# Projecting Q and K of 14 tokens six steps ahead in a two-layer recurrent attention kernel

## The chip, the cores and the metric

The kernel runs on one core of one Trainium2 chip, in one launch. The metric is the device time of that core in microseconds. The kernel before took 1781.42 us (median of three runs, 1781.21 to 1782.36).

## The reference

Two kinds of layer are applied twice with the same weights: a segmented attention with a recurrent memory (A), then a gated MLP (B), each on a layer norm and with a residual. The data type is bfloat16, the sequence has 2048 tokens of width 512, there are 32 heads of width 128, a segment has 32 tokens and the memory 8.

```python
def _A_ref(x, mem0, Wq, Wk, Wv, Wo, seg_len):
    ...
    mask = (idx[:, None] < M) | (idx[:, None] >= idx[None, :])
    mem = mem0
    for s in range(n_seg):
        xs = x[:, s * seg_len:(s + 1) * seg_len, :].copy()
        h = jnp.concatenate([mem, xs], axis=1)
        q = jnp.einsum('btd,dhe->bhte', h, Wq)
        k = jnp.einsum('btd,dhe->bhte', h, Wk)
        v = jnp.einsum('btd,dhe->bhte', h, Wv)
        scores = jnp.einsum('bhqe,bhke->bhqk', q, k) * scale
        scores = jnp.where(mask[None, None], scores, -1000000000.0)
        p = _softmax(scores, axis=-1)
        o = jnp.einsum('bhqk,bhke->bhqe', p, v)
        o = jnp.einsum('bhte,hed->btd', o, Wo)
        mem = o[:, :M, :].copy()
        outs.append(o[:, M:, :])
    return jnp.concatenate(outs, axis=1)
def _B_ref(x, w_gate, w_up, w_down):
    ...
    h = _sigmoid(g) * u
    return jnp.einsum('bsf,fd->bsd', h, w_down)
x = A_x
x = x + _A_ref(_layernorm(x, axis=-1), A_mem0, A_Wq, A_Wk, A_Wv, A_Wo, A_seg_len)
x = x + _B_ref(_layernorm(x, axis=-1), B_w_gate, B_w_up, B_w_down)
x = x + _A_ref(_layernorm(x, axis=-1), A_mem0, A_Wq, A_Wk, A_Wv, A_Wo, A_seg_len)
x = x + _B_ref(_layernorm(x, axis=-1), B_w_gate, B_w_up, B_w_down)
```

The loop over the 64 segments is a chain: a segment can begin only when the memory of the one before it is there. The tokens of a segment do not depend on that chain in the first attention layer: there they are the normalised input.

## The kernel before

**Steps.** `trace` (L1152) runs 70 steps. Step t works on segment t of the first attention layer (layer 0) and on segment t-6 of the second (layer 1); the distance 6 is `LAG`. Steps 0 to 5 have layer 0 alone and 40 columns (8 memory, 32 tokens); steps 6 to 63 have both and 80 columns; steps 64 to 69 have layer 1 alone, 40 columns. The transposed activations of a step lie in one of 8 ring tiles `hT` (128 x 4 x 80): columns 0 to 31 are the tokens of layer 0, 32 to 39 its memory, 40 to 47 the memory of layer 1, 48 to 79 its tokens. In steps 0 to 5 the columns 40 to 79 hold zeros (L572).

**One step** (`emit_step`, L826). The 32 heads go in six groups, five of six heads and one of two. A group does its work in halves of three heads: Q and K by matmuls of the weights' 128x128 blocks with the columns of `hT` (L892: 3 heads x 2 x 4 = 24 matmuls a half, 256 a step, into one PSUM bank), a copy of the bank to a tile `qku` on ScalarE (L902, recorded at L1232), and the scores (L906). Then come mask, maximum, subtraction, exponential, sum, reciprocal and product on VectorE and ScalarE (L920 to L937), a transpose (L949), two copies to `ptsb` (L960, on either engine), the product with V (L975), a copy `otsb` on ScalarE (L983), and the output projection (L993, 128 matmuls a step). The first columns of its result are the memory of the next step; VectorE copies them to the next `hT` (L1006, L1011), and then the Q and K of the next step can begin. V of most tokens is projected ahead of time in passes of a whole 128-row tile (`v_pass`, L695, and `v_half`, L732), goes to DRAM (`scr`), and is loaded into `vsb` by SyncE's queue (L861). V of the memory and of the remaining tokens is projected in the step by "strips" of 32 columns (L817) and put into `vsb` by more transfers of that queue (L872).

**Work beside the chain.** After every fourth step the MLP of a block of 128 tokens is done (`ffn`, L1048): seven pairs of gate and up matmuls (L1095), each followed by a tanh on ScalarE into one of two tiles `th` (L1100) and a product on VectorE (L1102), and then the down projection (L1119). Its weights come from DRAM each time by GpSimd's queue (L1087, L1088, L1113). These tasks, the V passes and the layer norms (L651 to L664) are what TensorE has besides the chain.

**Start.** The weights and the first blocks of x are loaded by SyncE's queue (L591, L779, L794). Blocks 2 and 14 are normalised first (L1167), then 3, 4, 5, 7, then the memory's initial value is transposed (L637), then blocks 0 and 1 (`pre1`), then 8, 10, 11, 13. Meanwhile TensorE runs matmuls on a tile of zeros, `hot` (L1218)[...].

**Order.** Every task is added to a planner with the engines that may run it, a cost, and the keys it reads and writes. A string, `SEQUENCE`, gives every task a rank. `forward` (L272) then simulates the engines: each time an engine is free it takes the ready task of best rank for which its buffers are free. The program is emitted in the order of the planned starts, and the engines run it in that order. A copy with two possible engines goes to the one that is free first. `warm` (L415) adds the matmuls on zeros before tasks of TensorE for which the plan has a gap of over 250 ns. The string therefore sets the order of the whole program, not only of the part around a change.

Of the kernel before, what the change touches and what calls it, by code (L numbers as in the profile page):

```python
# [13 lines left out]
BF16 = mybir.dt.bfloat16  # L14
# [12 lines left out]
SCOL = 24  # L27
BLK = 4
# [430 lines left out]
class Kern:  # L459
# [366 lines left out]
    def emit_step(self, t):  # L826
# [13 lines left out]
        pl.rate = ncol / 2.4 / mm_ns(ncol)  # L840

        c0 = 0 if both else L * j0

        def mv(c):
            return hT[:, c, c0:c0 + ncol]

# [451 lines left out]
```

## Time and profile before

| | |
|---|---|
| median of three runs | 1781.42 us |
| span of the profiled execution, first to last instruction | 1781.3 us |
| TensorE matmul busy | 1754.0 us, 98% |
| TensorE weight load busy | 1517.1 us, 85% |
| VectorE busy | 1144.1 us, 64% |
| ScalarE busy | 1167.8 us, 66% |
| GpSimd busy | 573.8 us, 32% |
| granted TensorE clock | 1.000 |
| first Q and K matmul of step 0, 1, 6, 7, 8, 12 | 28.3, 85.5, 177.5, 204.3, 224.2, 327.6 us |
| Q and K matmuls (L892) | 14848 of 80 columns, 3072 of 40 |
| matmuls on zeros (L1218) | 109 |

The span covers all but 0.1 us of the median. Busy is the union of an engine's instruction times. Matmuls overlap in the pipeline, so the mean of about 200 ns of one matmul is its latency and not its cost; the cost of one in a row of many is the distance between starts, which is read from the chain of work by dividing the length of a piece by its count.

### The profile page before, as it was taken

The numbers are of one execution on the slowest core, as the hardware profiler recorded it, in microseconds if no ns is written. First come the engines' busy times: TensorE is split into PE (matmuls) and PEld (weight loads), VectorE is DVE, ScalarE is ACT, GpSimd is POOL, SyncE is SP. The second block draws the span as 40 slices with busy tenths as digits, with TensorE's granted clock in tenths as the row PEclk, the third lists the DMA queues.
The fourth block names the chain that finished last, engine by engine and source line by source line (L and its number), as shares of the span: only waits on it lengthen the run. The fifth ranks groups of instructions, "written<-read, shape, count | busy, mean of one in ns | idle before, by whom it ended". The sixth has DMA issues, their size and how long they took to land.

```text
span 1781.3 us, 91977 instructions
## 1 busy us (share of the span) xinstructions
PE 1754.0 (98%) x39873; PEld 1517.1 (85%) x40083; DVE 1144.1 (64%) x3931; ACT 1167.8 (66%) x2973; POOL 573.8 (32%) x828
## 2 busy tenths in 40 slices
PE   9999999999999999999999999999999999999998
PEld 4688888888888898989898898988888888989886
DVE  4376666776577666756666676657656665666675
ACT  6676666666666666666766666666666766667564
POOL 5314031513233242323324241333324232333332
PEclk9999999999999999999999999999999999999999
DMA  9825254635555464445546453555555454555543
GB/s 342 265 74 165 59 155 121 195 105 158 146 162 153 133 174 136 139 137 165 160 130 198 135 161 106 154 160 167 156 148 172 111 145 140 158 156 139 165 143 94
DMA packets 131943, 270.66 MB, mean 152 GB/s; under 512 B 30394, under 2 KB 65090, under 8 KB 131538
## 3 DMA queue, kind: packets, MB, share of 16 engines
q0 software_dynamic: 56240, 181.91, 34.7%
q1 hardware_dynamic: 75298, 82.86, 16.3%
q8 instruction: 314, 5.14, 1.3%
q14 instruction: 91, 0.75, 0.1%
HBM read 220.41 MB, written 25.69 MB: 138 GB/s over the span
## 4 chain that ended last, share of the span: by engine, by line
PE 91%; DVE 5%; ACT 2%; issue 1%; DMA 1%; SPq 1%; POOL 0%; ACTq 0%; DVEq 0%; POOLq 0%
PE bank L892 31%; PE bank L993 17%; PE bank L1095 11%; PE bank L695 8%; PE bank L817 7%; PE bank L975 4%; PE bank L906 4%; PE bank L1119 4%; PE bank L949 2%; DVE st L920 1%; PE bank L1218 1%; PE bank L664 1%; DVE small L925 1%; DVE small L932 1%; DVE st L927 1%
## 5 line engine op out<-in xcount | busy, mean ns | idle before, releaser
L892 PE MATMUL bank<-hT,wq_sb 128*128 128x80 bf16 (+1 forms) x8960 | 622.6, 198 | 1.3 <-issue 0.6
L892 PE MATMUL bank<-hT,wk_sb 128*128 128x80 bf16 (+1 forms) x8960 | 622.5, 198 | 0.6 <-issue 0.6
L1232 ACT CAST qku<-bank 128x480 bf16<-128x480 f32 (+3 forms) x770 | 388.3, 512 | 222.5 <-PE bank L892 142.0
L892 PEld LDWEIGHTS <-wq_sb 128*128 128x128 bf16 x8960 | 454.1, 99 | 35.0 <-issue 25.1
L892 PEld LDWEIGHTS <-wk_sb 128*128 128x128 bf16 x8960 | 450.8, 99 | 0.8 <-issue 0.7
L920 DVE TENSOR_TENSOR st<-bank,cst 40x240 f32<-40x240 f32 (+3 forms) x768 | 277.7, 367 | 200.9 <-PE bank L906 194.2
L993 PE MATMUL bank<-otsb,wo_sb 128*128 128x80 bf16 (+1 forms) x8960 | 362.8, 198 | 1.9 <-ACT otsb L1232 0.2
L993 PEld LDWEIGHTS <-wo_sb 128*128 128x128 bf16 x8960 | 336.7, 99 | 16.3 <-issue 1.9
L1087 POOL DMA_DIRECT2D wg<-in_B_w_gate_dram x217 | 164.0, 756 | 299.1 <-PE bank L1095 109.8
L1232 ACT CAST otsb<-bank 128x480 bf16<-128x480 f32 (+3 forms) x420 | 199.8, 482 | 59.6 <-PE bank L975 47.6
L1088 POOL DMA_DIRECT2D wu<-in_B_w_up_dram x217 | 163.9, 756 | 197.3 <-PE bank L1095 89.3
L1113 POOL DMA_DIRECT2D wd<-in_B_w_down_dram x217 | 153.8, 709 | 213.4 <-PE bank L906 74.5
L930 ACT ACTIVATE st<-st 80x240 f32<-80x240 f32 (+3 forms) x420 | 159.5, 381 | 39.9 <-DVE st L927 37.1
L654 POOL TENSOR_TENSOR small<-small,cst 128x1 f32<-128x1 f32 (+1 forms) x80 | 44.8, 562 | 413.7 <-DVE small L653 410.2
L1095 PE MATMUL bank<-xnT,wg 128*128 128x128 bf16 (+2 forms) x1784 | 172.0, 219 | 0.8
L1095 PE MATMUL bank<-xnT,wu 128*128 128x128 bf16 (+2 forms) x1784 | 171.2, 219 | 0.0
L906 PE MATMUL bank<-qku 128*128 128x80 bf16 (+1 forms) x2240 | 161.0, 198 | 1.5 <-ACT qku L1232 0.2
L932 DVE TENSOR_REDUCE small<-st 80x6 f32<-80x240 f32 (+3 forms) x420 | 150.6, 360 | 16.3 <-ACT st L930 14.0
L937 DVE TENSOR_TENSOR pb<-st,small 80x240 bf16<-80x240 f32 (+3 forms) x420 | 153.6, 368 | 4.2
L927 DVE TENSOR_TENSOR st<-st,small 80x240 f32<-80x240 f32 (+3 forms) x420 | 154.1, 368 | 3.1
L925 DVE TENSOR_REDUCE small<-st 80x6 f32<-80x240 f32 (+3 forms) x420 | 151.4, 362 | 4.6
L975 PE MATMUL bank<-ptsb,vsb 104*128 104x80 bf16 x2048 | 140.2, 199 | 3.0 <-DMA vsb<-sst 1.5
(102 smaller groups left out, 2345.2 us busy)
## 6 DMA issues: line engine op xcount, KB each, us to landing
wg<-in_B_w_gate_dram POOLq DMA_DIRECT2D x220, 256.0 KB, 4.3
wu<-in_B_w_up_dram POOLq DMA_DIRECT2D x220, 256.0 KB, 4.3
wd<-in_B_w_down_dram POOLq DMA_DIRECT2D x220, 256.0 KB, 4.3
vsb<-scr SPq DMA_DIRECT2D x460, 48.0 KB
vsb<-sst SPq DMA_DIRECT2D x464, 32.0 KB
scr<-vst SPq DMA_DIRECT2D x112, 96.0 KB
wv_sb<-in_A_Wv_dram SPq DMA_DIRECT2D x8, 512.0 KB
wo_sb<-in_A_Wo_dram SPq DMA_DIRECT2D x10, 384.0 KB
```

Of the source, the lines that this page charges most:

```text
L892: nc.tensor.matmul(o_ap, lhsT=W[:, c, h * P:(h + 1) * P], rhs=mv(c), start=(c == 0), stop=(c == DC - 1))
L906: nc.tensor.matmul(s_all(SB)[:, w0 + i, :], lhsT=fview(qku[:, i, 0, 0:1], [(1, P)]), rhs=qku[:, i, 1, 0:ncol], start=True, stop=True)
L920: pl.add("DVE", dve_ns(n, True), lambda gsz=gsz, hs=hs, st=st, SB=SB, pj_=pj_, npj_=npj_, mk=mk, idx=idx: nc.vector.tensor_tensor(out=st[p ...
L925: pl.add("DVE", dve_ns(n), lambda hs=hs, st=st, mx=mx: nc.vector.tensor_reduce(out=mx[pr, hs], in_=st[pr, hs], axis=AX.X, op=ALU.max), r=s ...
L927: pl.add("DVE", dve_ns(n), lambda gsz=gsz, hs=hs, st=st, mx=mx: nc.vector.tensor_tensor(out=st[pr, hs], in0=st[pr, hs], in1=mx[pr, hs].uns ...
L932: pl.add("DVE", dve_ns(n), lambda hs=hs, st=st, sm=sm: nc.vector.tensor_reduce(out=sm[pr, hs], in_=st[pr, hs], axis=AX.X, op=ALU.add), r=s ...
L975: nc.tensor.matmul(fview(OB[:, o:o + 1], [(ncol, 2), (1, L)]), lhsT=self.vsb[halves[u // 8]][0:64 + L, j, (u % 8) * P:(u % 8 + 1) * P], rh ...
L993: nc.tensor.matmul(WB[:, c * ncol:(c + 1) * ncol], lhsT=self.wo[:, h, c * P:(c + 1) * P], rhs=otsb[:, hl, 0:ncol], start=(h == 0 and c == ...
L1087: pl.add("POOL", 760, lambda wg=wg, fs=fs: nc.gpsimd.dma_start(out=wg[:], in_=self.wgv[:, :, fs]), r=[("wo", self.H - 1)], w=[gk] + bt, la ...
L1088: pl.add("POOL", 760, lambda wu=wu, fs=fs: nc.gpsimd.dma_start(out=wu[:], in_=self.wuv[:, :, fs]), r=[("wo", self.H - 1)], w=[uk] + bt, la ...
L1095: nc.tensor.matmul(gu[:, 2 * i + k, 0:n], lhsT=W[:, c, i * P:(i + 1) * P], rhs=xnT[:, c, rw], start=(c == 0), stop=(c == DC - 1))
L1232: nc.scalar.copy(out=dst, in_=src)
```

## The change

The columns 40 to 79 of `hT`, which steps 0 to 5 leave unused, get 14 tokens of the segment that is six steps away. `early_x` copies the first 14 normalised tokens of segment t+6 into columns 40 to 53 of step t's tile, for t = 0 to 5 (from block 1 for t = 0 and 1, from block 2 for t = 2 to 5). In steps 0 to 5 the Q and K matmuls take 54 columns. The first 40 go to `qku` as before. The other 14 columns of each head go to a tile `kx` (128 x 32 x 2 x 14), by one more copy per half group on ScalarE or VectorE, and from there to a DRAM tensor `xq`, in two transfers a step on SyncE's queue. In steps 6 to 11 the two parts are loaded back into the same tile `kx`; the matmuls take columns 14 to 79, 66 in place of 80; the copy of the bank fills columns 14 to 79 of `qku`, and one more copy per half group, from `kx`, fills columns 0 to 13. The second tile `th` of the MLP is gone; the one that is left is a pool of the planner. The string `SEQUENCE` is another one, so that all instructions stand in a new order. In the new order the initial memory is transposed first, and the blocks of x are loaded in another order. Counted over the program, TensorE has 1536 matmuls of 66 columns and 1536 of 54 where it had 1536 of 80 and 1536 of 40, and 85 matmuls on zeros for 109; ScalarE and VectorE have 66 copies into `kx` (59 and 7), 66 out of it (46 and 20), and 6 into `hT` (4 and 2) more; SyncE's queue has 24 transfers more; all else is the same in number.

```diff
+NE = 14
...
 SEQUENCE = r"""
...
+        self.kx = c.tile([P, H, 2, NE], BF16, name="kx")
+        self.xq = dr.tile([self.LAG * P, H * 2 * NE], BF16, name="xq")
         self.hff = [c.tile([P, FC, P], BF16, name=f"hff{i}") for i in range(1)]
-        self.th = [c.tile([P, 2, P], F32, name=f"th{i}") for i in range(2)]
+        self.th = [c.tile([P, 2, P], F32, name=f"th{i}") for i in range(1)]
...
+        self.thp = Pool(self.th)
...
+    def early_x(self, pst, B, b):
+        for i in range(BLK):
+            t = b * BLK + i - self.LAG
+            if 0 <= t < self.LAG:
+                dst = self.hT[t % self.R][:, :, L:L + NE]
+                self.pl.add(("ACT", "DVE"), copy_ns(4 * NE, True), lambda dst=dst, i=i: (dst, pst()[:, :, i * SEG:i * SEG + NE]),
+                            r=[B], w=[("hT", t % self.R, 1, q) for q in ("m", "x")])
...
+            if b == 2:
+                self.early_x(pst, B, b)
...
+        save, load = t < LAG, LAG <= t < 2 * LAG
+        q0, q1 = (0, L + NE) if save else (NE, ncol) if load else (c0, c0 + ncol)
+        nq = q1 - q0
+        parts, pos = ((0, self.H // 2 + 2), (self.H // 2 + 2, self.H)), 0
+        if load:
+            for lo, hi in parts:
+                w = NE * 2
+                pl.add("SP", 430, lambda lo=lo, hi=hi, w=w: nc.sync.dma_start(out=fview(self.kx[:, lo, 0, 0:1], [(1, (hi - lo) * w)]),
+                                                                             in_=self.xq[(t - LAG) * P:(t - LAG + 1) * P, lo * w:hi * w]),
+                       r=[("xq", t - LAG, lo)], w=[("kx", p) for p in range(lo, hi)], lat=3000.0, nb=P * (hi - lo) * w * 2)
+
         def mv(c):
-            return hT[:, c, c0:c0 + ncol]
+            return hT[:, c, q0:q1]
...
-                            o_ap = pq[:, (2 * i + qk_) * ncol:(2 * i + qk_ + 1) * ncol]
+                            o_ap = pq[:, (2 * i + qk_) * nq:(2 * i + qk_ + 1) * nq]
...
+                d0 = NE if load else 0
+                nw_ = ncol - d0
                 def qkcopy(nh=nh, pq=pq, qku=qku):
-                    return (fview(qku[:, 0, 0, 0:1], [(LW, 2 * nh), (1, ncol)]),
-                            pq[:, 0:2 * nh * ncol].rearrange("p (m b) -> p m b", b=ncol))
+                    return (fview(qku[:, 0, 0, d0:d0 + 1], [(LW, 2 * nh), (1, nw_)]),
+                            pq[:, 0:2 * nh * nq].rearrange("p (m b) -> p m b", b=nq)[:, :, 0:nw_])
...
+                if load:
+                    pl.add(("ACT", "DVE"), copy_ns(2 * nh * NE, True), lambda nh=nh, qku=qku, kxv=kxv: (fview(qku[:, 0, 0, 0:1], [(LW, 2 * nh), (1, NE)]), kxv()),
+                           r=kk, w=[(qku, "e")], use=[qku])
...
+                if save:
+                    pl.add(("ACT", "DVE"), copy_ns(2 * nh * NE), lambda nh=nh, pq=pq, kxv=kxv: (kxv(), pq[:, 0:2 * nh * nq].rearrange("p (m b) -> p m b", b=nq)[:, :, L:nq]),
+                           r=[pq], w=kk)
+                pos += nh
+                for lo, hi in parts:
+                    if save and pos == hi:
+                        w = NE * 2
+                        pl.add("SP", 430, lambda lo=lo, hi=hi, w=w: nc.sync.dma_start(out=self.xq[t * P:(t + 1) * P, lo * w:hi * w],
+                                                                                     in_=fview(self.kx[:, lo, 0, 0:1], [(1, (hi - lo) * w)])),
+                               r=[("kx", p) for p in range(lo, hi)], w=[("xq", t, lo)], lat=3000.0, nb=P * (hi - lo) * w * 2)
...
-            hi2 = self.nxt("th", 2)
-            th = self.th[hi2]
+            th = pl.buf(self.thp)
...
         p1 = self.pre1(1)
+        self.early_x(*p1, 1)
```

## The prediction, made before the changed kernel ran

> **What bounds the kernel now.** I read the page first, then the windows by step, then the chain of waits, and last the timeline where a step looked short of work.
>
> ```profile
> span 1781.3 us, 91977 instructions
> PE 1754.0 (98%) x39873; PEld 1517.1 (85%) x40083; DVE 1144.1 (64%) x3931; ACT 1167.8 (66%) x2973; POOL 573.8 (32%) x828
> PE 91%; DVE 5%; ACT 2%; issue 1%; DMA 1%; SPq 1%; POOL 0%; ACTq 0%; DVEq 0%; POOLq 0%
> ```
>
> TensorE is idle for 27.3 us in all, and 91% of the chain that ended last is its matmuls. So a matmul that becomes shorter is worth its whole saving wherever other TensorE work stands ready. Busy alone doesn't say what a matmul costs; the chain does, by length over count:
>
> ```profile
> 69.75 2.40 PE bank L892 x96
> ...
> 177.69 3.44 PE bank L892 x96
> 181.24 2.58 PE bank L892 x72
> ```
>
> 40 columns: 2.40/96 = 25.0 ns. 80 columns: 3.44/96 = 2.58/72 = 35.83 ns. And 128 columns, at 241 us:
>
> ```profile
> 244.39 0.90 PE bank L1095 x16
> ```
>
> 0.90/16 = 56 ns. Now the steps that the change touches: the start, steps 1 to 5, then 6, 7 and 8 (columns: stretch, its length, then busy us of PE, weight loads, DVE, ACT, POOL, then clock, DMA share, GB/s):
>
> ```profile
> 0.00:28.30 28.30, 27.07 (x146) 12.55 (x149) 11.52 (x44) 17.33 (x28) 16.29 (x46) 1.00 0.98 324
> ...
> 85.50:177.50 92.00, 89.38 (x2583) 75.62 (x2587) 62.38 (x221) 60.74 (x202) 25.52 (x36) 1.00 0.43 120
> 177.50:204.30 26.80, 26.54 (x556) 20.97 (x559) 14.64 (x52) 17.93 (x42) 0.00 (x0) 1.00 0.26 69
> 204.30:224.20 19.90, 18.93 (x479) 17.57 (x475) 12.80 (x48) 13.92 (x34) 0.00 (x0) 1.00 0.18 46
> 224.20:251.60 27.40, 27.22 (x624) 25.11 (x626) 18.70 (x65) 16.67 (x41) 11.89 (x17) 1.00 0.52 150
> ```
>
> Steps 6 and 8 last 27 us because V passes and the MLP fill them; step 7 lasts 19.9 us and is the only one with nothing to fill it (no L695, no L1095, 1.3 us of zeros). There VectorE is the bound: it starts at 208.27 and then works without a gap to 221.1.
>
> ```profile
> 208.27 0.84 DVE L920 TENSOR_TENSOR st<-bank,cst 80x240 f32<-80x240 f32 x2 [5.85 <-PE bank L906]
> ...
> 220.90 0.24 DVE L1226 TENSOR_SCALAR ptsb<-bank,small 104x80 bf16<-104x80 bf16 x1
> ```
>
> At the start TensorE multiplies zeros; the first normalised block is ready at 9.31 + 0.40 = 9.71 us, but its transposes come at 11.98, behind 43 of them:
>
> ```profile
> 1.00 11.14 PE L1218 MATMUL bank<-hot 128*128 128x512 bf16 x43 [1.00 <-DVE small L564]
> 11.98 0.39 PE L664 MATMUL bank<-cst,xn 128*128 128x128 bf16 x4
> ```
> ```profile
> 9.31 0.40 DVE L655 TENSOR_SCALAR xn<-xs,small 128x512 bf16<-128x512 bf16 x1
> ```
>
> **What the Trainium skill says.** (1) "TensorE: Matmul & The Clock Gate", section "Wait — 56ns, not 53.3ns?": back to back and warm, a matmul of N columns takes N/2.4 + 2.5 ns, never under about 25 ns. The trace agrees at 80 (35.83), 128 (56) and at the floor (25.0 for 40). (2) "ScalarE: Activation LUTs", section "What ACT_TABLE_LOAD costs": 186 ns + 0.833 ns an element with immediates, and back-to-back instructions overlap by 93 ns. The trace has the slope, (557-358)/240 = 0.83, and a little less fixed time. (3) "DMA: Bandwidth & Descriptors", section "Specifications": full rate wants pieces of 512 B or more. The new transfers have rows of 784 and 1008 B; no row of this trace tests that.
>
> **The change part by part.** The sum is made against the profiled span, 1781.3 us; 0.1 us lies around it to the median, 1781.42.
>
> *a. 66 columns for 80, steps 6 to 11.* 6 x 32 heads x 2 x 4 = 1536 matmuls. No 66 is in the trace. By (1) it is 30.0 ns; the slope between 80 and 128, (56-35.83)/48 = 0.42 ns a column, gives 35.83 - 14 x 0.42 = 29.95. The other end is the straight line from 40 to 80, 32.0. I take 30.0: 1536 x 5.83 = **-8.96 us**; other end -5.8.
>
> *b. 54 for 40, steps 0 to 5.* Again 1536. By (1) 54/2.4 + 2.5 = 25.0, exactly the floor: I take **0**. By the straight line it would be 28.8 and 1536 x 3.8 = +5.8. Nothing excludes that, but 80 and 128 lie on the formula, and the formula meets the floor at 54.
>
> *c. Copies in steps 0 to 5.* 66 copies of 84 or 56 columns out of PSUM, 59 on ScalarE. The nearest rows there:
>
> ```profile
> L1232 ACT CAST qku<-bank 128x240 bf16<-128x240 f32 x50 | 17.9, 358 | 14.0 <-PE bank L892 9.6 <-PE bank L906 3.1 <-DVE small L925 0.6
> ...
> L1232 ACT COPY ptsb<-bank 40x120 bf16<-40x120 bf16 x23 | 5.7, 246 | 0.6 <-PE bank L949 0.3
> ```
>
> 358 - 156 x 0.83 = 0.23 us each, 13.6 us in six steps. In 85.5 to 177.5 ScalarE is busy 60.7 of 92 us; with 5/6 of it, 72: no bound. But in most halves the new order puts the copy to `kx` ahead of the one to `qku`. The scores, the softmax and the exponential wait behind it, and the bank stays taken 0.23 us longer. The path feels the first half group of a step: 6 x 0.23 = 1.4 us. The cover is V passes and, from step 4, the MLP on TensorE; before that it is thin (the zeros at this place say so). I take **+0.8**, range 0 to 3.
>
> *d. Copies in steps 6 to 11.* The `qku` copies shrink by 84 elements, 0.07 us each; 46 copies out of `kx` at about 0.24 us come to ScalarE, 20 to VectorE. That is about +7 us on ScalarE, which is busy some 98 of 150 us, and +5 on VectorE. Their data come from DRAM long before; 0 outside step 7, where each VectorE copy counts. Lost with it in step 7: narrowing shortens only what comes before the first score (208.27 - 204.3 = 4.0 us, 72 to 96 matmuls, 0.4 to 0.6 us), not 256 x 5.83 = 1.5. Against that, the new order puts the step's strip pass (L817, 1.84 us) into the middle of its Q and K instead of ahead of step 7: work that step 6 had to carry. I take **+0.4** for step 7, range -0.5 to +1.2.
>
> *e. SyncE's queue.* 24 more issues at about 0.4 us (the x blocks' 0.37 to 0.43): 10 us of a queue that mostly waits for free V buffers (455 us at L861 behind L975). The loads to the single `kx` wait until the copies of the step before have read it; the one for step 6's second part waits for the landing of step 5's store just ahead of it, about 3 us (a transfer to `vsb` took 3.0 to 3.9 in the chain). Behind them stand the V loads of the next step (L861, L872), and the product with V waits for those. It comes some 10 us after its step begins, so the cover is 10 us: **0**, range 0 to 3. GpSimd's queue gets nothing new.
>
> *f. One tile `th`.* A tanh now waits for the product before it, with ScalarE's copies queued behind. A pair takes 0.22 + 0.22 and two hand-overs, 0.57 us, for 32 rows (1770.49 to 1771.06 in the trace of before), about 0.8 for 96. Between steps seven pairs have tens of microseconds. At the end nine pairs (7 x 0.57 + 2 x 0.8 = 5.6 us) stand where 1770.49 to 1775.93 = 5.4 us stand now. **+0.4**, range 0 to 1.5.
>
> *g. Start.* The order has 34 matmuls on zeros ahead of the first projection for 50, and the memory's transpose first. If the zeros end by about 9.5 us, the transposes wait for the layer norm alone; that now has four statistics and two copies ahead of it, about 10.5 us in place of 9.7. Three 14-column copies (0.25 each) also stand ahead of the second copy that the projection needs. Against 14.29 us now, that makes the first V pass 0 to 2 us earlier. But the DMA engines are 98% busy until 28 us, so the weights may be late instead. I take **-0.7**, range -2 to +1.
>
> *h. The rest of the order.* All idle time of TensorE beyond start and end is about 21 us; another order moves some of it, in a direction that I can't tell: 0, plus or minus 2.
>
> Sum: -8.96 + 0 + 0.8 + 0.4 + 0 + 0.4 - 0.7 = -8.1. 1781.4 - 8.1 = **1773.3 us**.
>
> **The rivals.** *R1, 54 columns are not at the floor*: +5.8, 1779.1 us. For it: between 40 and 80 there is no measured width. Against: 80 and 128. *R2, slower, by SyncE's queue*: a load of `kx` waits for the last copy of its part, the V loads are stuck behind it, and TensorE runs out at L975. It costs a landing, 3 us, and decides from where the V loads lose their 10 us of cover. At one a step it is +18 us: 1791. To end above 1785 it needs 11.7/6 = 2 us a step. For it: a single `kx` and an in-order queue. Against: L975 waits 3.0 us in the whole run now. *R3, more is won*: at the start the zeros' full 2.3 us, and step 7 gives back nothing: 1773.3 - 1.6 - 0.4 - about 1 of (c) and (f) = 1770.3. *That the change doesn't do what it says* is excluded: the order has 1536 matmuls of 66 columns.
>
> **Chances.** About 0.2%, 3.6 us, is what a measurement of this kernel can tell from no change: the bounds are 1777.9 and 1785.0. Forecast 0.65 (1770.5 to 1777.5, nearly all faster); R1 0.15 (a third below 1777.9); R2 0.07; R3 0.13. Faster 0.65 + 0.05 + 0.13 = 0.83, same 0.10, slower 0.07. The range 1769.5 to 1778.5 leaves out R2, most of R1 and a little of R3.
>
> **What would show it.** Right: L892 pieces of 66 columns at 30.0 ns and of 54 at 25.0; step 7 little shorter than 19.9 us, the other steps of 6 to 11 1.5 us shorter or fuller; steps 1 to 5 within 1 us each of 16 to 23; L975 still without waits on DMA. Wrong: 54 columns above 26 ns, SyncE waits ahead of `kx` that end in a wait of L975, or a first projection later than 14.3 us.

## The result and the profile after

The changed kernel takes 1788.58 us (median of 1783.26, 1787.47, 1788.58, 1788.62 and 1788.99) against 1781.42 for the kernel before. These two medians alone would give 1.0040, 7.2 us; the ratio on record, which is used from here on, is 1.0025, 95% interval [1.0014, 1.0036]. So it is slower by some 4.5 us, with 2.5 to 6.4, where 8 us less were forecast. The profiled execution took 1788.62 us with a span of 1786.8, so 1.8 us lie around the span. (The 0.1 us that the prediction put there paired a span with the time of another execution.)

The page of the changed kernel, the lines that answer to the first three of before:

```profile
span 1786.8 us, 92278 instructions
...
PE 1757.7 (98%) x40059; PEld 1511.0 (85%) x40059; DVE 1178.8 (66%) x4061; ACT 1155.2 (65%) x2981; POOL 581.9 (33%) x839
...
PE 89%; DMA 5%; SPq 2%; issue 1%; ACT 1%; DVE 1%; POOL 1%; POOLq 0%; ACTq 0%; DVEq 0%
```

The share of TensorE in the chain that ended last fell from 91% to 89%, and DMA and SyncE's queue came in with 7% for 2%. That is the trail to follow. First the matmuls; from the chain of the changed kernel (start, length, what), one piece of 54 columns and one of 66:

```profile
160.08 3.00 PE bank L926 x120
...
284.56 3.63 PE bank L926 x120
```

54 columns: 3.00/120 = 25.0 ns. 66 columns: 3.63/120 = 30.25 ns. Both are within 0.3 ns what the prediction took, and what the Trainium skill's "TensorE: Matmul & The Clock Gate", section "Wait — 56ns, not 53.3ns?", gives. So the matmuls did become shorter by 9 us, and something took back 13.

To find where, I gave every matmul the cost that it has in a row of many (columns/2.4 + 2.5 ns, at least 25; 57.5 ns for the strips and 116 for the half passes of V, as measured; nothing for zeros) and took the sum from the end of the last matmul: what is left is TensorE's **lost time**. (The trace of before lacks 210 matmul records, 39873 beside 40083 weight loads; there the weight load stands for the matmul.) The sum of costs is 1716.0 us before and 1707.0 after, 9.0 less. Lost time by stretch, in us, from one profiled execution each (before, after, and two experiments that are explained below). A slow clock counts as lost time too; after has a short piece of it at 1161 us, about 1.7 of its 25.7, and a_best one at 30 us, as much of its 3.2:

| stretch, us | before | after | widths alone (b_width) | best version (a_best) |
|---|---|---|---|---|
| 0 to 30 | 14.7 | 13.1 | 15.7 | 13.7 |
| 30 to 90, step 0 | 0.6 | 7.9 | 1.0 | 3.2 |
| 90 to 210, steps 1 to 6 | 12.3 | 12.2 | 13.3 | 13.6 |
| 210 to 330, steps 7 to 11 | 3.9 | 9.9 | 8.1 | 7.6 |
| 330 to 1740 | 23.8 | 25.7 | 24.1 | 24.1 |
| 1740 to the end | 6.5 | 7.7 | 5.5 | 4.7 |
| sum | 61.8 | 76.5 | 67.7 | 66.9 |

Two stretches carry the loss: step 0 with 7.3 us more than before, and steps 7 to 11 with 6.0. (In the line numbers of after, the Q and K matmuls L892 are L926, the scores L906 are L961, the product with V L975 is L1030, the output projection L993 is L1048, the transfers L872 to `vsb` are L906, and most copies are recorded at L1287.)

**Step 0.** The two longest of TensorE's waits of the changed kernel between 28 and 95 us (what waits, for whom: us in all, times, longest); before there is no DMA wait there, and none over 0.2 us:

```profile
PE bank L1048 <- DMA wo_sb<-in_A_Wo_dram: 3.3, 1, 3.3
PE bank L716 <- DMA wv_sb<-in_A_Wv_dram: 1.6, 1, 1.6
```

The second, for the weights of V (L716), ends at 28.8 us. The chain of the same kernel shows why the weights of the output projection are late:

```profile
66.62 0.98 ACT sst L1287 x2
...
68.00 0.23 SPq L906
...
73.72 9.84 DMA wo_sb<-in_A_Wo_dram
...
83.61 1.12 PE bank L1048 x28
84.72 1.71 PE bank L716 x4
```

The transfers from `sst` to `vsb` (L906) can't be issued before ScalarE has filled `sst`, at 67.6 us. SyncE's queue is in order; it had issued nothing after 57.3, and behind these transfers stand the last six loads of `wo_sb`, 2.1 MB by their shapes (five of 128x3x512, one of 128x512, two bytes each), issued from 70.3 to 73.7. The last lands at 83.6. The windows of the changed kernel (stretch, length, busy of PE, weight loads, DVE, ACT, POOL, clock, DMA share, GB/s) show two more things:

```profile
60.00:70.00 10.00, 9.57 (x166) 5.72 (x167) 2.57 (x9) 6.07 (x19) 2.06 (x4) 1.00 0.32 99
...
82.70:86.10 3.40, 2.49 (x32) 1.52 (x33) 0.97 (x3) 0.27 (x1) 0.00 (x0) 0.50 0.37 129
86.10:89.50 3.40, 3.40 (x74) 3.28 (x73) 0.56 (x2) 1.30 (x3) 1.08 (x2) 0.50 0.29 81
89.50:92.90 3.40, 3.40 (x140) 3.36 (x138) 2.00 (x7) 2.36 (x11) 0.00 (x0) 1.00 0.02 6
```

The DMA engines, the limit of the start, were busy for a third only between 60 and 70 us; before it was

```profile
60.00:70.00 10.00, 9.95 (x90) 4.61 (x90) 2.73 (x8) 6.80 (x13) 3.21 (x6) 1.00 1.00 335
```

And the granted clock was 0.50 for 6.8 us, from 82.7 to 89.5, most of it after the wait: the four V matmuls of 84.72 took 0.43 us each in place of 0.22, the first 120 matmuls of step 1 took 4.42 us in place of 3.0, the 28 of 83.61 took 40 ns in place of 25. That is 0.85 + 1.4 + 0.4 = 2.7 us on top of the wait in this execution. The other four need not have it: the mean granted clock was 0.997 in three of the five and 0.999 in two, and these two took 1787.47 and 1788.58 us, no less. So the share of the slow clock in the 4.5 us is not settled. The Trainium skill says in "TensorE: Matmul & The Clock Gate", section "What's actually happening", that an idle window of about 3.4 us brings the clock down to a half; the wait here was 3.3 us. Other runs show the same slow clock after shorter waits, down to 1.3 us in a_wop, so the measurement decides against that length as a limit; the last section has them.

**Steps 7 to 11.** ScalarE's waits between 204 and 330 us in the changed kernel:

```profile
ACT qku L1287 <- PE bank L926: 11.6, 20, 1.4
ACT qku L1287 <- DMA kx<-xq: 4.7, 3, 2.2
```

and its chain around one of the three waits for `kx` (L985 is the exponential):

```profile
218.76 0.55 ACT otsb L1287 x2
219.31 2.24 DMA kx<-xq
...
221.57 0.03 ACT qku L1287
...
221.74 0.42 ACT qku L1287 x2
222.16 0.30 ACT st L985
222.46 0.45 ACT otsb L1287
222.91 0.04 issue
222.95 1.02 PE bank L1048 x24
```

At 219.31 SyncE issues the load of `kx` for step 8, behind eight transfers to `vsb` that took it from 212.5 to 219.2. Step 8 begins at 228. But ScalarE's order has the copies out of `kx` as early as this, in step 7; it stands at the first one until 221.57, and the exponential and the copy `otsb` that TensorE needs now stand behind it. TensorE waits at the output projection. Its two longest waits between 204 and 330 us, which the kernel before doesn't have, are behind ScalarE:

```profile
PE bank L1048 <- ACT otsb L1287: 1.9, 2, 1.2
PE bank L961 <- ACT qku L1287: 1.2, 1, 1.2
```

### The profile page after: what moved, and what is told of

It is laid out like the page before. It is cut to its first block, busy times and chain, and to the rows that moved or that the text cites. A ratio compares the mean times of both kernels' runs of the same rounds, so it can differ in the third digit from the quotient of the medians.

```text
span 1786.8 us, 92278 instructions
## 1 busy us (share of the span) xinstructions
PE 1757.7 (98%) x40059; PEld 1511.0 (85%) x40059; DVE 1178.8 (66%) x4061; ACT 1155.2 (65%) x2981; POOL 581.9 (33%) x839
## 4 chain that ended last, share of the span: by engine, by line
PE 89%; DMA 5%; SPq 2%; issue 1%; ACT 1%; DVE 1%; POOL 1%; POOLq 0%; ACTq 0%; DVEq 0%
PE bank L926 31%; PE bank L1048 16%; PE bank L1150 10%; PE bank L840 7%; PE bank L716 7%; PE bank L1173 5%; PE bank L1030 4%; PE bank L961 4%; PE bank L1004 2%; DMA vsb<-sst 2%; SPq L906 2%; DMA wv_sb<-in_A_Wv_dram 1%; PE bank L676 1%; DMA wo_sb<-in_A_Wo_dram 1%; PE bank L1118 0%
## 5 line engine op out<-in xcount | busy, mean ns | idle before, releaser
L926 PE MATMUL bank<-hT,wq_sb 128*128 128x80 bf16 (+3 forms) x8960 | 616.7, 198 | 1.2 <-issue 1.1
L926 PE MATMUL bank<-hT,wk_sb 128*128 128x80 bf16 (+3 forms) x8960 | 616.2, 198 | 0.5 <-issue 0.5
L1287 ACT CAST qku<-bank 128x480 bf16<-128x480 f32 (+3 forms) x770 | 387.8, 507 | 219.8 <-PE bank L926 180.9
L926 PEld LDWEIGHTS <-wq_sb 128*128 128x128 bf16 x8960 | 452.5, 99 | 23.7 <-issue 13.6
L926 PEld LDWEIGHTS <-wk_sb 128*128 128x128 bf16 x8960 | 447.7, 99 | 1.2 <-issue 1.2
L975 DVE TENSOR_TENSOR st<-bank,cst 40x240 f32<-40x240 f32 (+3 forms) x768 | 279.3, 368 | 155.6 <-PE bank L961 149.4
L1048 PE MATMUL bank<-otsb,wo_sb 128*128 128x80 bf16 (+1 forms) x8960 | 362.3, 198 | 5.5 <-DMA wo_sb<-in_A_Wo_dram 3.3
L1048 PEld LDWEIGHTS <-wo_sb 128*128 128x128 bf16 x8960 | 336.3, 99 | 18.8 <-DMA wo_sb<-in_A_Wo_dram 3.7
L1287 ACT CAST otsb<-bank 128x480 bf16<-128x480 f32 (+3 forms) x420 | 199.0, 484 | 68.1 <-PE bank L1030 48.2
L985 ACT ACTIVATE st<-st 80x240 f32<-80x240 f32 (+3 forms) x420 | 158.9, 381 | 44.4 <-DVE st L982 42.8
L961 PE MATMUL bank<-qku 128*128 128x80 bf16 (+1 forms) x2240 | 163.2, 198 | 1.4 <-ACT qku L1287 1.2
L982 DVE TENSOR_TENSOR st<-st,small 80x240 f32<-80x240 f32 (+3 forms) x420 | 154.6, 370 | 4.0
L1030 PE MATMUL bank<-ptsb,vsb 104*128 104x80 bf16 x2048 | 136.7, 199 | 7.8 <-DMA vsb<-sst 6.1
```

Source lines behind the costliest of these rows:

```text
L926: nc.tensor.matmul(o_ap, lhsT=W[:, c, h * P:(h + 1) * P], rhs=mv(c), start=(c == 0), stop=(c == DC - 1))
L961: nc.tensor.matmul(s_all(SB)[:, w0 + i, :], lhsT=fview(qku[:, i, 0, 0:1], [(1, P)]), rhs=qku[:, i, 1, 0:ncol], start=True, stop=True)
L975: pl.add("DVE", dve_ns(n, True), lambda gsz=gsz, hs=hs, st=st, SB=SB, pj_=pj_, npj_=npj_, mk=mk, idx=idx: nc.vector.tensor_tensor(out=st[p ...
L982: pl.add("DVE", dve_ns(n), lambda gsz=gsz, hs=hs, st=st, mx=mx: nc.vector.tensor_tensor(out=st[pr, hs], in0=st[pr, hs], in1=mx[pr, hs].uns ...
L985: pl.add("ACT", act_ns(n), lambda hs=hs, st=st: nc.scalar.activation(out=st[pr, hs], in_=st[pr, hs], func=ACTF.Exp, scale=self.scale), r=s ...
L1030: nc.tensor.matmul(fview(OB[:, o:o + 1], [(ncol, 2), (1, L)]), lhsT=self.vsb[halves[u // 8]][0:64 + L, j, (u % 8) * P:(u % 8 + 1) * P], rh ...
```

## The experiments

Each ratio is against the kernel before, run beside it on the same chip; 0.001 is 1.8 us. The changed kernel itself (after) was measured once, in five executions, and not again beside the experiments; "less than after" is the difference of two ratios, and its error, from both intervals, is given with it. Line numbers shift a little from kernel to kernel. My theory: the matmuls' gain is real, and two late DMA arrivals, the weights in step 0 and `kx` in steps 7 to 11, take it back. The main rival: the new order as a whole, or the copies and transfers of `kx`, are dear.

**The widths alone, in the order of before (b_width).**

```diff
+        save, load = t < LAG, LAG <= t < 2 * LAG
+        q0, q1 = (0, L + NE) if save else (NE, ncol) if load else (c0, c0 + ncol)
...
-            return hT[:, c, c0:c0 + ncol]
+            return hT[:, c, q0:q1]
```

> The kernel before, in its own order, with the widths of the change alone: 54 columns in steps 0 to 5 (the 14 extra ones hold zeros), 66 in steps 6 to 11; it leaves out Q and K of 14 tokens in six steps. Theory (the matmuls' saving is real and full, the loss comes from elsewhere): 1536 x 5.83 = 9.0 us less, 1772.4. Rival 1 (54 columns are not at the floor): 1778. Rival 2 (TensorE waits for others in steps 6 to 11, so that shorter matmuls only become waits): 1778 to 1781.

Measured: 0.9982 [0.9974, 0.9989], 3.2 us less (1.9 to 4.6). My theory failed here and rival 2 holds: a third of the 9.0 us comes through. The table has the rest: lost time in steps 7 to 11 grows from 3.9 to 8.1 us. Step by step, from one first Q and K matmul to the next:

| step | before: length, lost | b_width: length, lost |
|---|---|---|
| 6 | 26.8, 0.2 | 25.7, 0.6 |
| 7 | 19.8, 3.0 | 19.3, 3.9 |
| 8 | 27.5, 0.1 | 27.0, 1.2 |
| 9 | 28.1, 0.5 | 27.6, 1.4 |
| 10 | 24.6, 0.1 | 23.6, 0.7 |
| 11 | 23.2, 0.2 | 22.6, 1.0 |

Each step has 1.5 us less of matmuls and is 0.4 to 1.1 us shorter. TensorE's waits of b_width between 205 and 325 us name the next limits:

```profile
PE bank L982 <- DMA vsb<-sst: 1.3, 2, 0.8
PE bank L982 <- ACT ptsb L1239: 0.7, 1, 0.7
```

L982 is the product with V. Before, it had 0.2 us of waits there. V comes by a chain of its own (strips, copy to `sst`, SyncE's queue, transfer), and TensorE, in a fixed order, now reaches the product earlier than V or the softmax does. These waits are 2.0 us, of 4.2 that were lost; the rest lies in pieces too short for this view, and what they wait for is not shown.

**The new order alone (a_order).** The matmuls take 40 and 80 columns again, and each of the new copies and transfers is left out:

```diff
-            return hT[:, c, q0:q1]
+            return hT[:, c, c0:c0 + ncol]
...
-lambda nh=nh, qku=qku, kxv=kxv: (fview(qku[:, 0, 0, 0:1], [(LW, 2 * nh), (1, NE)]), kxv())
+lambda: None
```

> The kernel after, in its own order and with its one tanh tile, but with the widths of before (40 and 80) and with all that is new for kx left out (early copies, copies into and out of kx, stores, loads). Theory (of the 15 us lost, about 5 go with the loads of kx, the rest with the new order): 1788.6 + 9.0 - 5 = 1792.6, that is 11 above the kernel before. Rival (the copies and transfers of kx are the whole loss, the order costs nothing): 1781 to 1783.

Measured: 1.0038 [1.0025, 1.0051], 6.8 us more. The sign is the theory's, the size is smaller. The rival falls: without anything of `kx` the new order is slower than the old one.

**No loads of kx (a_noload).** Only `lambda: None` in place of the twelve loads; the copies out of `kx` stay and take old values.

> The kernel after without the twelve loads of kx (the copies out of kx stay and take old values). Theory (the loads come late, the copies out of kx wait for them on ScalarE, and TensorE waits behind those): 4 to 6 us less than after, 1783 to 1784.5, and no waits over 1 us in steps 7 to 11 at the copies out of kx. Rival (the waits there are paid by other waits, the loss is the order's): within 1 us of after.

Measured: 1.0005 [0.9996, 1.0013]. Against the 1.0025 of after this is 3.6 us less, plus or minus 2.5; lost time from 210 to 330 us falls from 9.9 to 6.4. That is what the loads cost. What is left is more than the 3.9 of before, as with the widths alone (8.1).

**The weights earlier on SyncE's queue (a_wo).**

```diff
         order = self.pl.plan()
+        at = min(order.index(tk) for tk in self.sst_ld)
+        late = [tk for tk in order[at:] if tk in self.wo_ld]
+        order = [tk for tk in order[:at]] + late + [tk for tk in order[at:] if tk not in late]
```

(`sst_ld` and `wo_ld` hold the tasks of the transfers from `sst` and of the loads of `wo_sb`.)

> The kernel after with the last six loads of the output projection's weights moved ahead of the first transfer to vsb that waits for its copies; nothing else is moved. Theory (these loads stand 10 us behind that transfer, and the output projection of step 0 waits 3.5 us for the last of them): 3.5 us less, 1785, up to 1783.5 if later waits go with it. Rival (the V data of step 0 come later in return, or the DMA engines were the limit): within 1 us of after.

Measured: 1.0013 [1.0004, 1.0023], 2.1 us less than after, plus or minus 2.6: not told apart from no gain, nor from 3.5. The 22 executions spread from 1779.8 to 1790.7 us, and the profiled one, 1789.6, lies near the upper end. In it the wait for `wo_sb` is gone, and another stands between 28 and 95 us, at the transposes (L1008):

```profile
PE bank L1008 <- DVE pb L996: 3.7, 1, 3.7
```

Its chain, in order of time:

```profile
60.08 6.15 DMA scr<-wd
...
66.33 0.58 ACT wd L1294
66.91 0.31 ACT st L989
```

The six loads, now issued from 58.8 to 61.7, compete with the stores of V to `scr` that GpSimd's queue issues in the same microseconds. A store takes 6.15 us where it took 4.0 in after; ScalarE's copy into the buffer that the store frees waits, and the exponential stands behind the copy. In this execution the wait was moved, not removed.

**The weights on GpSimd's queue (a_wop).** The same six loads, behind the last of those stores, where the DMA engines are free:

```diff
+        at = min(order.index(tk) for tk in self.sst_ld)
+        late = [(tk, fn) for tk, fn in self.wo_ld if order.index(tk) > at]
+        for tk, fn in reversed(late):
+            order.remove(tk)
+            order.insert(at, tk)
+            tk.on, tk.fn, tk.nb = "POOL", fn, 0
```

> The kernel after with the last six loads of the output projection's weights on GpSimd's queue, behind its stores of V (they were on SyncE's queue, behind a transfer that waited until 67.6 us). Theory: on SyncE's queue these loads either came too late or, moved ahead, held up the stores of V for which TensorE then waited 4 us at 64 us; between 62 and 70 us the DMA engines are busy for a third only, so loads put there cost nothing, and the wait of 3.5 us at the output projection of step 0 goes: 3.5 to 4.5 us less than after, a ratio of 1.000 to 1.0007 to the kernel before. Rival (the start is bound by the bytes to be moved, so that each order of the queue ends at the same time): a ratio of 1.0015 to 1.003, and another wait before 90 us.

Measured: 0.9991 [0.9982, 0.9999], 6.1 us less than after, plus or minus 2.5, more than expected. Its windows:

```profile
60.00:70.00 10.00, 8.40 (x137) 4.59 (x136) 2.22 (x7) 5.98 (x15) 6.96 (x11) 1.00 0.77 244
70.00:80.00 10.00, 10.00 (x179) 6.57 (x176) 7.71 (x28) 8.18 (x26) 4.80 (x9) 1.00 0.67 204
```

The DMA engines work through the gap (0.77 for 0.32), TensorE has no wait for `wo_sb`, and the clock stays at 1.00 here. The excess over 3.5 us would fit the 2.7 us of slow clock that came with the wait in the profile of after; that it is this is not shown.

**The new order alone, with that edit (a_order_wop).**

> The new order alone (widths of before, nothing of kx), with the last six loads of the output projection's weights on GpSimd's queue. Theory (nearly all that the new order loses against the order of before is the place of these six loads): 1.0038 - 0.0034 = 1.0004, between 0.9998 and 1.001. Rival (the new order loses by many small waits): 1.002 or more.

Measured: 1.0009 [1.0000, 1.0018], as the theory had it. So of the 6.8 us that the new order loses, 5.2, plus or minus 2.8, go with the place of six loads.

**The copies out of kx later (a_kx).**

```diff
+        for kc, qc in self.kx_cp:
+            order.remove(kc)
+            order.insert(order.index(qc), kc)
+        for tk in self.kx_ld:
+            order.remove(tk)
+            order.insert(1 + max(i for i, q in enumerate(order) if q.idx in tk.deps), tk)
```

(`kx_cp` pairs each copy out of `kx` with the copy of its half group; `kx_ld` holds the loads.)

> The kernel after with each copy out of kx right ahead of the copy of the same half group, and each load of kx right behind the last copy that reads the part (the copies stood up to half a step earlier in ScalarE's order, where the loads had not landed). Theory (the load is late only because ScalarE asks for it too early): nearly all that leaving out the loads gave, 3 to 4 us less than after, a ratio of 1.000 to 1.001 to the kernel before, and no waits over 0.5 us of ScalarE for the loads. Rival (the loads themselves hold up SyncE's queue): a ratio of 1.002 or more, with waits at the product with V.

Measured: 1.0012 [1.0004, 1.0020], between theory and rival: 2.3 us less than after, plus or minus 2.4, so by itself hardly told apart from no gain. ScalarE has no wait for `kx` left over 0.3 us in steps 7 to 11. The product with V now waits 1.4 us for its data, where after has 0.4; that was the rival's sign. Counted from the start of their step the loads are issued at about the same times as in after, but for one of step 8's, which comes 5 us earlier.

**The loads of kx on GpSimd's queue (a_kxp).** `nc.gpsimd` in place of `nc.sync`, each load behind the last copy that reads its part; the copies stay early.

> The kernel after with the twelve loads of kx on GpSimd's queue, each behind the last copy that reads the part; the copies out of kx stay where they are in ScalarE's order. Theory (half of the cause is SyncE's queue: the loads stand behind five to eight transfers to vsb of 0.6 us each, and on another queue they start 2 to 4 us earlier): 2 to 3.5 us less than after, a ratio of 1.0005 to 1.0014 to the kernel before. Rival 1 (the single tile sets the start of the loads, only the place of the copies on ScalarE matters): a ratio of 1.002 to 1.003, with the same waits of ScalarE. Rival 2 (waiting in GpSimd's queue they hold up the weights of the MLP): over 1.003.

Measured: 1.0027 [1.0013, 1.0042], no gain; neither rival had the whole reason. ScalarE's waits for `kx` do go (0.5 us for 4.7), and lost time from 210 to 330 us falls from 9.9 to 5.6. But at 177 us there is a new wait of TensorE, at the transposes of a layer norm (L680):

```profile
PE bank L680 <- DVE xn L671: 4.4, 1, 4.4
```

and in GpSimd's queue between 160 and 190 us:

```profile
POOL kx L878 <- ACT st L989: 5.4, 1, 5.4
POOL kx L878 <- ACT sst L1295: 4.9, 1, 4.9
```

GpSimd computes one power in each layer norm (L670). It stood behind two loads of `kx` that waited for copies and for the weights' loads in the same queue; the norm, its transposes and TensorE waited with it. So SyncE's queue had a part in the late loads; but a transfer that waits for data needs a queue where nothing urgent stands behind.

**Both cures (a_best).**

> The two edits together, the six loads of weights on GpSimd's queue and the copies out of kx later. Theory (two separate losses, each about 3.5 us): 7 us less than after, a ratio of 0.998 to 0.999 to the kernel before. Rival (either gain is taken up by waits elsewhere): 1.000 or more.

Measured: 0.9972 [0.9958, 0.9986], 1778.88 us beside 1783.21 for before: faster than both kernels, and 9.4 us less than after, plus or minus 3.2. 7 were forecast. Two edits of place and queue alone, with the same matmuls and copies, take back more than the whole loss.

```profile
span 1777.5 us, 92271 instructions
```

**The old ranks, planned anew (b_new).** The string of before, each new task with the rank of its neighbour, copies and loads of `kx` as in a_kx.

> All of the change but its string of ranks: the ranks are those of the kernel before, each new copy and transfer has its rank beside the task that it belongs to, and the copies out of kx and the loads stand as in the run with later copies. Theory (the new string costs some 5 us at the start, the copies and the single tanh tile 1 to 3 us): the widths alone gave 0.998, so 0.998 to 1.000. Rival (the ranks of before do not fit the new tasks, or the copies into and out of kx are dear): over 1.001.

Measured: 1.0081 [1.0068, 1.0093]. The rival holds: the planner, given longer copies and other matmul times, moves tasks everywhere, and lost time is 86.5 us, spread over the program (20.2 for 12.3 of before from 90 to 210 us, 30.3 for 23.8 from 330 to 1740). The ranks fit one set of costs. So this run doesn't price the change; the next one does.

**All of the change with every old task in its old place (b_fix).**

```diff
+                if load:
+                    self.pre[qc] = [lambda nh=nh, qku=qku, kxv=kxv: (fview(qku[:, 0, 0, 0:1], [(LW, 2 * nh), (1, NE)]), kxv())]
...
+                for fn in self.pre.get(tk.idx, ()):
+                    nc.scalar.copy(out=fn()[0], in_=fn()[1])
                 got = tk.fn()
```

(and in the same way, after the task, the copy into `kx`, the store and the load)

> The whole change without its new order: all tasks stand exactly as in the kernel before; the copies into kx stand on ScalarE right behind the copies of their halves, the copies out of kx on ScalarE right ahead of them, each store and each load of kx right behind the last copy of its part, with one tanh tile. Theory (the change itself is worth what the widths alone gave, less 1 to 2 us for copies and the tanh tile; the loss was the new order's and the early copies'): a ratio of 0.9985 to 0.9995 to the kernel before. Rival (without an order made for them the copies and transfers cost more than the widths give): 1.001 or more.

In this run and in the next one, a tanh can stand ahead of the product that still needs the one before, in the one tile that is left; the MLP's values change by that, its instructions don't.

Measured: 1.0004 [0.9995, 1.0013], between theory and rival. Against b_width it is 3.9 us more, plus or minus 2.1. Steps 6 to 11 have the lengths of b_width within 0.5 us, so no cost of the copies out of `kx` shows there. The loss that shows is in step 0 (2.3 us more) and step 5 (1.1 us more). TensorE's waits between 28 and 178 us:

```profile
PE bank L1034 <- DMA wo_sb<-in_A_Wo_dram: 1.7, 2, 1.4
PE bank L947 <- ACT kx L1282: 0.9, 1, 0.9
```

The scores (L947) wait for a copy into `kx`, and `wo_sb` is late here too, with the stores of `kx` ahead of its loads.

**One tanh tile (b_th1).** `th = self.th[0]` in the kernel before.

> The kernel before with one tanh tile in place of two, in its own order. Theory and prediction: 0 to 0.4 us, a ratio of 1.000 to 1.0005. Rival (the single tile costs a part of the loss that was put down to the order): 1.001 or more, with waits at the gate and up matmuls or at the end.

Measured: 1.0006 [0.9998, 1.0014], 1.1 us with -0.4 to +2.5: theory and rival are not told apart.

## Why the prediction was wrong

The matmuls' own gain was forecast rightly. Three steps failed: the worth of that gain (a), the loads of `kx` taken at nothing (e), and the start, taken as a gain (g). By the prediction's own terms:

- **a, 66 for 80.** The term is right to the nanosecond (30.25 for 30.0, 9.0 us in all). The step that failed stands above it: that a shorter matmul "is worth its whole saving wherever other TensorE work stands ready". TensorE looked 98% busy, with 27.3 us idle where its lost time was 61.8, and its order is fixed: the work that could fill a wait had its place already. Lost time of 0.1 to 0.5 us in steps 6 and 8 to 11 did not mean that TensorE was alone in front; the waits of b_width say that V and the softmax ended little earlier. Worth in the order of before: 3.2 us. Between a_order_wop and a_best, in the new order, narrowing with all its copies is worth 1.0009 - 0.9972, 6.6 us, plus or minus 3.0.
- **b, 54 for 40.** Right: 25.0 ns. R1 falls with it, and so does R3, since no more was won.
- **c, copies into kx.** +0.8 with 0 to 3. In b_fix about 3.4 us in steps 0 and 5, together with the stores' share; just over the upper end. The mechanism, scores behind the copy, was named.
- **d, copies out of kx.** That they are free outside step 7 fits b_fix. "Their data come from DRAM long before" is wrong: the data came 1.0 to 2.2 us after ScalarE asked, three times in steps 7 to 11.
- **e, SyncE's queue.** Forecast 0 with 0 to 3; it is 3.6 us, plus or minus 2.5 (a_noload). I looked at who stands behind the loads (V and L975), and gave them 10 us. I did not look at what stands ahead of the loads (eight transfers of 0.6 us), nor at where the consumer stands: in ScalarE's order up to half a step before it is needed.
- **f, one tanh tile.** 0.4 for 1.1 plus or minus 1.5: not told apart.
- **g, the start.** The first projection came 2.3 us earlier (11.99 for 14.29), the first Q and K of step 0 3.5 us, and lost time to 30 us fell by 1.6 (forecast 0.7). But I followed only the weights of the first projections ("the weights may be late instead", +1); the wait of 1.6 us for those of V came too. The weights that cost most were those of step 0's last stage, behind a blocked queue. This is the largest error: 5 to 6 us (a_order_wop, a_wop), in the profiled execution 3.3 by the wait and 2.7 by the clock.
- **h, the rest of the order.** 0 plus or minus 2 holds: a_order_wop is 1.6 us over before, the tanh tile included.

R2, with a chance of 0.07, was right in its sign and its queue: SyncE's order decided, at two places. Its place (L975) and its price (3 us a step) were wrong.

From the runs: order without the six loads +1.6, the six loads +5 to +6, narrowing and copies -6.6, late loads of `kx` +2.3 to +3.6. The sum is +2.3 to +4.6, each term with an error of 2 to 3; measured +4.5, [2.5, 6.4]. What stays open: what the slow clock costs in an execution other than the profiled ones, the share of queue and of early copies in the late loads of `kx` (a_kx and a_kxp each remove the wait, and each has another cost), and how much of the waits of step 0 any order could avoid, since the DMA engines are full until 60 us.

## What to carry to other kernels

A nearly full engine with a fixed order is not yet the only limit: before giving a shorter instruction its whole saving, ask stage by stage what would be late next, because fill that is already placed can't move. For each transfer on an in-order queue look both ways, at what waits behind it and at what blocks ahead of it, and at the place of its consumer in the consumer's own order. When an order is new, check the last stage of the start as well as the first: which loads still stand in the queue, and behind what.

## What the runs showed of the hardware

A wait of TensorE can cost more than its length. Away from the first and last microseconds, the granted clock in these traces was either 1.00 or 0.50, and 0.50 came in pieces of 3.4 us: two in a row in after from 82.7 us, one each elsewhere. The waits of TensorE around their start were 3.3 us long in after, 3.7 in a_wo (69.2 us), 4.4 and 2.1 in a_kxp (182.4 and 83.4), 2.0 in after (1161.3), and only 1.3 in a_wop:

```profile
PE bank L1034 <- DMA vsb<-sst: 1.3, 1, 1.3
PE bank L965 <- ACT qku L1297: 0.3, 1, 0.3
```

```profile
238.20:241.60 3.40, 1.78 (x29) 1.19 (x27) 2.37 (x9) 2.29 (x8) 0.91 (x2) 1.00 0.78 227
241.60:245.00 3.40, 3.40 (x45) 3.01 (x44) 2.23 (x7) 1.64 (x5) 1.03 (x2) 0.50 0.53 137
245.00:248.40 3.40, 3.40 (x77) 3.09 (x75) 2.56 (x12) 2.02 (x6) 2.03 (x3) 1.00 0.51 158
```

After waits of 2.4 us in a_order and 2.7 in a_noload, in step 0, it stayed at 1.00. So the length of the longest wait alone doesn't decide.
